# Order of the first layer's products in tiles 2 to 6 of an attention and MoE kernel

## The chip, the cores and the metric

The kernel runs on one core of a Trainium2 chip. Its time is the device time of one execution, in microseconds (us). Times given for several executions are medians. One further execution was recorded by the hardware profiler; the durations below come from it.

The engines are TensorE (PE, matrix products; PEld are its weight loads), VectorE (DVE), ScalarE (ACT), GpSimd (POOL) and SyncE (SP). Each works through its own list of instructions in order; one that needs another engine's result waits for a semaphore, and all behind it on the same engine wait too. TensorE writes to PSUM banks, here tiles of 128 x 512 f32.

## The reference

```python
q, k, v: (8, 8, 576, 64)           # batch, heads, positions, head dimension
kv  = einsum('bhsd,bhse->bhde', k, v)
out = einsum('bhsd,bhde->bhse', q, kv)
rms = sqrt(mean(out * out, axis=-1, keepdims=True) + 1e-06)
x   = (out / rms * g_norm)  as rows of 512: (4608, 512)
h   = x @ w_in                      # 512 -> 2048
g   = h * (1 / (1 + exp(-1.702 * h)))
y   = g @ w_out                     # 2048 -> 512
```

All inputs and the output are f32; the kernel multiplies in f16 and accumulates in f32.

## The kernel before, in words

**Tiles.** The 4608 rows of x are worked in nine tiles (`NT`) of 512 rows. Tiles 0 to 7 hold 512 rows of one batch each, tile 8 the 64 rows left over of every batch. The attention for tile t + 1 runs between the products of tile t's second layer, so TensorE goes from layer to layer without a pause for it. A tile's x is made by `turn` (L356): VectorE scales the rows, and a transposing DMA from SP's queue (L365) brings them to x with the columns on the partitions, in two DMAs: rows 0 to 255 of the tile (the first half of x's columns as the layers read it) and rows 256 to 511 (the second half).

**Two layers by seven products.** From tile 1 on each layer is a 2 x 2 block product done with seven block products instead of eight (Winograd's form of Strassen's method). For the first layer the weights' sums are in `ws`, made once. The sums of x are made in each tile by `Sums.form` (L505, line L509) on VectorE: four f16 arrays in the tile `xS`, 128 x 512 each. With x's quarters b11, b12 (upper half of the 512 features, first and second half of the columns) and b21, b22 (lower half), they are

- form(0): b12 - b11, "the difference of the halves", needed by product 5
- form(1): b22 - form(0), needed by product 6
- form(2): b22 - b12, needed by product 7
- form(3): b21 - form(1), needed by product 4

Products 1 and 2 use b11 and b21 only, thus only the first half of the columns. Product 3 uses b22.

**Steps.** The 16 column blocks of the hidden layer are in four groups (0 to 3). A step is written as two digits, the group and the product: "25" is product 5 of group 2. Each is four matmuls of 128 x 128 weights and 256 columns (line L577), two row blocks by two blocks of 128 features. The order of the steps is written out by hand in a `Plan`: `SECOND` (L928) for tile 1, `LATER` (L941) for tiles 2 to 6, `LAST_TWO` (L954) for 7 and 8. A group has three banks:

- x takes product 1, then adds 6, 7 and 4
- y starts as a copy of x after product 1 (the "snapshot"), then adds product 2
- z takes product 5; product 5 is also copied to `s5` in SBUF; when 5 and 6 are both done, z becomes x + s5 (an addition on VectorE, L591); then product 3 adds to z

After product 7 VectorE forms s5 = x + s5 (L593). The results y (after 2), z (after 3), s5 (after 7) and x (after 4) each go through the activation on ScalarE (`gate`, L555, line L557) into gT, the second layer's input.

`copy` (L526, line L527) makes the snapshots and the copies to s5, on the engine that the plan's `snap` names for each group: in LATER product 1 'DAAA' (group 0 on DVE, the others on ACT) and product 5 'AAAD' (groups 0, 1 and 2 on ACT). `xsums` gives the step behind which each `form` is issued, `ready` the step behind which the second layer's sums are formed.

**Order of issue.** `hid_seven` (L733) walks through the steps. A step's matmuls are issued first, then its copy or addition. The gate that a step returns is kept back, and issued behind the next step's matmuls and copies. So on ACT the gate of step n stands behind the copy of step n + 1.

**Banks.** Three pools hold the eight PSUM banks: ps_a (3), ps_h (3) and ps_o (2), lines L56 to L58. In LATER x of the groups 0 to 3 is in ps_a, ps_o, ps_o, ps_a, y always in ps_h, z in ps_a, ps_a, ps_h, ps_h. The second layer of the tile before holds both banks of ps_o until its end: one is emptied by an addition on DVE (L674), the other, the last, by a copy on ACT (L677).

Of the kernel before, what the change touches and what calls it, by code (L numbers as in the profile page):

```python
# [16 lines left out]
def kernel(  # L17
# [202 lines left out]
    class Attention:  # L220
# [3 lines left out]
        def __init__(self, b):  # L224
            self.b, self.kb = b, kvb[b] if b < EARLY else kvd[b % 2]
            self.qT, self.o = {}, {}
            x = xpool.tile([P, KO * SM], F16, name="xT", tag="xT")
            if b < EARLY:
                self.x = xT[b] = x.rearrange("p (c n) -> p c n", c=KO)
            else:  # L230
                self.x = x.rearrange("p (m r) -> p m r", r=P)
                xT[b] = x.rearrange("p (j c r) -> p c j r", j=J, c=KO)
# [65 lines left out]
        def product(self, t, c):  # L298
            nc.tensor.matmul(t, self.kb[:, c, :], self.qT[c][:, 0:SM], start=True, stop=True)  # L299
# [226 lines left out]
    def copy(engine, to, src):  # L526
        (nc.vector.tensor_copy if engine == "D" else nc.scalar.copy)(to, src)  # L527

    class SevenIn:


        def __init__(self, hid, xs, g, todo):
            self.snap = {p: e[g] for p, e in todo.snap.items()}
            self.pool = todo.pool[g]
            self.gT, self.xs, self.g, self.i = hid.gT, xs, g, PARTS[g]
            self.bank, self.done = {}, set()
            self.s5 = stage.tile([P, 2, TH], F32, name="s5", tag="s5")
# [28 lines left out]
        def product(self, p):  # L566

            name = {1: "x", 6: "x", 7: "x", 4: "x", 2: "y", 5: "z", 3: "z"}[p]  # L570
            if p in (1, 5):
                self.open(name)
            bank = self.bank
            for a in range(2):
                for k in range(KH):
                    w, x = self.operands(p, a, k)
                    nc.tensor.matmul(  # L577
                        bank[name][:, a],
                        w,
                        x,  # L580
                        start=(p in (1, 5) and a == 0 and k == 0),
                        stop=(k == KH - 1),
                        skip_group_check=True,
                    )
            self.done.add(p)
            if p == 1:
                copy(self.snap[1], self.open("y"), bank["x"])
            elif p == 5:
                copy(self.snap[5], self.s5, bank["z"])
            if p in (5, 6) and self.done >= {5, 6}:  # L590
                nc.vector.tensor_add(bank["z"], bank["x"], self.s5)  # L591
            elif p == 7:
                nc.vector.tensor_add(self.s5, bank["x"], self.s5)  # L593
                return lambda: self.gate(1, 1, self.s5)
            elif p in (2, 3, 4):
                r, n = {2: (0, 0), 3: (0, 1), 4: (1, 0)}[p]
                return lambda: self.gate(r, n, bank[name])
# [135 lines left out]
    def hid_seven(t, hid, seven, units1):  # L733
# [10 lines left out]
        for n, step in enumerate(todo.steps):  # L744
            behind, gates = gates, []
            if step != "kv":
                gate = product(step)
                if gate:
                    gates.append(gate)
            for u in behind:  # L750
                u()
            for u in units1.get(n, ()):
                u()
            for i in range(4):
                if todo.xsums[i] == n:
                    xs.form(i)
            for i0, i1, which in todo.ready.get(n, ()):
                seven.sums(i0, i1, which)
# [3 lines left out]
        def late(step):  # L762
            gate = product(step)
            if gate:
                gate()
# [144 lines left out]
    for fo in COLS[4:GROUP]:  # L910
# [28 lines left out]
        {'rows': (19, 19), 'add_up': (22, 26, 27, 31), 'table': 26, 'roots': (27, 33), 'turn': (40, 50, 51, 52)},  # L939
    )  # L940
    LATER = Plan(  # L941
# [4 lines left out]
        {1: 'DAAA', 5: 'AAAD'},  # L946
        "D",
        "aooa",
        "aahh",
        {15: '34'},  # L950
        (0, 1, 5, 10),
        {'rows': (15, 15), 'add_up': (17, 20, 24, 28), 'table': 24, 'roots': (28, 29), 'turn': (35, 38, 46, 48)},
    )
    LAST_TWO = Plan(  # L954
# [12 lines left out]
    def plan(t):  # L967
        return SECOND if t < EARLY else LATER if t < B - 1 else LAST_TWO
# [7 lines left out]
    for t in range(NT):  # L976
# [47 lines left out]
        elif b < B:  # L1024
            todo = plan(t)
# [78 lines left out]
```

## Time and profile before

| what | us |
|---|---|
| median of 3 executions | 258.92 |
| lowest and highest of them | 258.73, 259.25 |
| the profiled execution | 259.85 |
| its span, first to last instruction | 258.1 |
| PE busy in the span | 250.8 |
| DVE, ACT busy | 190.1, 180.2 |
| first layers of tiles 2, 3, 5 and 6, each | 11.80 |

The granted clock of TensorE was 1.000 of full speed over the span. In lists of groups a row gives line, engine, operation, output <- input, the count, the busy time and the mean in ns, and then the idle time of the engine in front of them with what ended it. In a timeline a row gives start and duration in us, engine, line, operation, and in brackets idle time in front. PE's rows overlap: a matmul's shown time holds its way through the array, and the next one starts before it ends. Times in the chain are start and length.

### The profile page before, as it was taken

What the parts mean: (1) busy time and instruction counts of PE and PEld (TensorE: products, weight loads), DVE (VectorE), ACT (ScalarE), POOL (GpSimd) and SP (SyncE); (2) the same over time, 40 slices, a digit from 0 to 9 for tenths busy, and PEclk for the clock granted to TensorE, in tenths of its full rate; (3) what the DMA queues carried; (4) which work ended last, traced back from release to release, by engine and by line L of the source; (5) the groups of instructions that cost most, each with busy time, mean ns of one, the idle gap of its engine ahead of it and who ended that gap; (6) DMA issues with size and microseconds to landing.
All of it is one profiled execution on the core that took longest, in us unless ns stands there. A gap on an engine that the chain in (4) does not pass through costs nothing.

```text
span 258.1 us, 6355 instructions
## 1 busy us (share of the span) xinstructions
PE 250.8 (97%) x2596; PEld 204.0 (79%) x2596; DVE 190.1 (74%) x339; ACT 180.2 (70%) x327; POOL 57.2 (22%) x91
## 2 busy tenths in 40 slices
PE   8889999999999999999899999999999999999994
PEld 2444554788888888888788888898888888888883
DVE  1565677899938794889469867986799787857872
ACT  3477725988769886988589958995899469536800
POOL 8872235116080103041160130200000000000013
PEclk9999999999999999999999999999999999999999
DMA  7999999999999986999999669986700430012005
GB/s 173 193 200 205 204 204 197 234 198 150 159 178 201 203 118 139 139 136 169 182 144 205 82 152 134 156 95 137 204 3 0 84 163 3 0 60 105 3 19 145
DMA packets 68671, 35.33 MB, mean 137 GB/s; under 512 B 37954, under 2 KB 66242, under 8 KB 68386
## 3 DMA queue, kind: packets, MB, share of 16 engines
q0 software_dynamic: 37616, 18.31, 55.6%
q1 hardware_dynamic: 30624, 16.29, 29.5%
q8 instruction: 20, 0.33, 0.5%
q10 hardware_dynamic: 402, 0.33, 0.4%
q14 instruction: 9, 0.07, 0.1%
HBM read 36.70 MB, written 9.44 MB: 179 GB/s over the span
## 4 chain that ended last, share of the span: by engine, by line
PE 89%; DMA 7%; DVE 1%; issue 0%; ACT 0%; POOL 0%; DVEq 0%
PE h L577 38%; PE o L697 36%; PE o L812 5%; PE hT L470 5%; DMA xT<-x 2%; DMA vbuf<-in_v_dram 2%; DMA qraw<-in_q_dram 2%; PE kvp L246 2%; PE outR L329 1%; PE ss L376 1%; DVE x L359 1%; PE outT L299 0%; PE q L451 0%; PE kvp L258 0%; DVE xT L386 0%
## 5 line engine op out<-in xcount | busy, mean ns | idle before, releaser
L557 ACT ACTIVATE gT<-h 128x512 f16<-128x512 f32 x96 | 52.3, 601 | 5.6 <-PE h L577 5.6
L577 PEld LDWEIGHTS <-ws 128*128 128x128 f16 x512 | 50.1, 98 | 7.0 <-issue 1.1
L577 PE MATMUL h<-xS,ws 128*128 128x256 f16 x384 | 53.0, 273 | 1.0 <-DVE xS L509 1.0
L697 PEld LDWEIGHTS <-gS 128*128 128x128 f16 x512 | 49.0, 98 | 6.2 <-DVE gS L629 0.3
L697 PE MATMUL o<-tw,gS 128*128 128x256 f16 x384 | 45.6, 273 | 0.0
L577 PEld LDWEIGHTS <-w_in_sb 128*128 128x128 f16 x384 | 37.5, 98 | 4.7
L697 PEld LDWEIGHTS <-gT 128*128 128x128 f16 x384 | 37.6, 98 | 4.3
L577 PE MATMUL h<-xT,w_in_sb 128*128 128x256 f16 x224 | 31.8, 273 | 0.0
L697 PE MATMUL o<-w_out_sb,gT 128*128 128x256 f16 x256 | 31.4, 273 | 0.0
L591 DVE TENSOR_TENSOR h<-h,s 128x512 f32<-128x512 f32 x32 | 22.3, 699 | 11.3 <-PE h L577 5.3
L674 DVE TENSOR_TENSOR osb<-o,qf 128x512 f32<-128x512 f32 (+1 forms) x25 | 16.7, 668 | 11.7 <-PE o L697 11.7
L593 DVE TENSOR_TENSOR s<-h,s 128x512 f32<-128x512 f32 x32 | 22.1, 691 | 4.4 <-PE h L577 3.3
L629 DVE TENSOR_TENSOR gS<-gT 128x512 f16<-128x512 f16 (+2 forms) x32 | 21.3, 685 | 0.6 <-ACT gT L557 0.6
L557 ACT ACTIVATE gT<-s 128x512 f16<-128x512 f32 x32 | 19.8, 628 | 2.6 <-DVE s L593 2.6
L731 POOL DMA_DIRECT2D out_dram<-osb x6 | 3.2, 540 | 82.5 <-DVE osb L674 82.5
L577 PE MATMUL h<-xS,w_in_sb 128*128 128x256 f16 x128 | 18.9, 272 | 0.0
L345 DVE TENSOR_REDUCE sum<-sq 128x8 f32<-128x512 f16 x24 | 14.9, 678 | 4.8 <-ACT sq L339 4.8
L984 ACT ACT_TABLE_LOAD x14 | 18.0, 1283 | 0.3
L317 ACT ACTIVATE sq<-outT 128x512 f16<-128x512 f32 (+1 forms) x16 | 7.8, 489 | 14.5 <-PE outT L299 8.9
L378 ACT ACTIVATE rs<-ss,eps_t 128x512 f32<-128x512 f32 (+1 forms) x16 | 9.2, 581 | 11.5 <-PE ss L376 11.4
L527 ACT COPY h<-h 128x512 f32<-128x512 f32 x27 | 15.4, 577 | 2.2 <-PE h L577 2.0
L577 PE MATMUL h<-xT,ws 128*128 128x256 f16 x112 | 16.8, 273 | 0.0
(104 smaller groups left out, 358.9 us busy)
## 6 DMA issues: line engine op xcount, KB each, us to landing
out_dram<-osb SPq DMA_DIRECT2D x8, 512.0 KB, 4.3
kraw<-in_k_dram POOLq DMA_DIRECT2D x5, 512.0 KB, 7.4
vbuf<-in_v_dram POOLq DMA_DIRECT2D x5, 512.0 KB, 10.2
out_dram<-osb SPq DMA_DIRECT2D x2, 1024.0 KB, 4.8
qraw<-in_q_dram POOLq DMA_DIRECT2D x3, 512.0 KB, 12.2
qbuf<-in_q_dram POOLq DMA_DIRECT2D x3, 512.0 KB, 6.0
out_dram<-osb SPq DMA_DIRECT2D x6, 192.0 KB, 5.7
w_in_sb<-in_moe_w_in_dram POOLq DMA_DIRECT2D x2, 512.0 KB, 9.8
```

The lines of the kernel that those rows point to most:

```text
L345: nc.vector.tensor_reduce(out=self.sum4[:, j, :], in_=self.o[j][1].rearrange("p (x d) -> p x d", d=D), op=ALU.add, axis=mybir.AxisListType.X,)
L470: nc.tensor.matmul(self.h[fo], w_in_sb[:, ko, fo * P : (fo + 1) * P], self.x[:, ko], start=(ko == 0), stop=(ko == KO - 1),)
L527: (nc.vector.tensor_copy if engine == "D" else nc.scalar.copy)(to, src)
L557: nc.scalar.activation(self.gT[:, to, n * TH : (n + 1) * TH], src, AFT.Gelu_apprx_sigmoid)
L577: nc.tensor.matmul(bank[name][:, a], w, x, start=(p in (1, 5) and a == 0 and k == 0), stop=(k == KH - 1), skip_group_check=True,)
L591: nc.vector.tensor_add(bank["z"], bank["x"], self.s5)
L593: nc.vector.tensor_add(self.s5, bank["x"], self.s5)
L629: op(s[:, n, lo], a, b)
L674: nc.vector.tensor_add(o, ps, self.kept[with_][:, m])
L697: nc.tensor.matmul(o, a, w, start=(p in (1, 2, 5) and i == 0 and (mo == 0 or split)), stop=(i == HF - 1), skip_group_check=True,)
L812: nc.tensor.matmul(os[mo], gT[:, fo, mo * P : (mo + 1) * P], w_out_sb[:, fo, :], start=(fo == 0), stop=(fo == FO - 1),)
L984: u2.setdefault(i, []).append(lambda: f(*args))
```

## The change

In the plan LATER the order of the first eight products is

- before: 21, 01, 25, 22, 05, 06, 11, 02
- after: 21, 01, 11, 22, 25, 05, 06, 02

and the rest stays. Four products (16 matmuls) that read only b11 and b21 stand before 25, the first that reads form(0); before it was two (8 matmuls). The snapshot of step 11 is not taken behind 11 but at a step of its own, written "10", between 06 and 02, so ps_h hands out its banks in the same order as before: y of group 2, y of group 0, z of group 2, y of group 1. A step with product 0 issues only the snapshot. form(1) is issued behind the first step with form(0), thus ahead of the snapshot of 01 on DVE. `ready` and the last two of `xsums` grow by one, since the plan has one step more, and mean the same places.

```diff
         def __init__(self, hid, xs, g, todo):
             self.snap = {p: e[g] for p, e in todo.snap.items()}
+            self.held = f"{g}0" in todo.steps
...
+            bank = self.bank
+            if p == 0:
+                copy(self.snap[1], self.open("y"), bank["x"])
+                return None
             name = {1: "x", 6: "x", 7: "x", 4: "x", 2: "y", 5: "z", 3: "z"}[p]
             if p in (1, 5):
                 self.open(name)
-            bank = self.bank
...
             self.done.add(p)
-            if p == 1:
+            if p == 1 and not self.held:
                 copy(self.snap[1], self.open("y"), bank["x"])
...
     LATER = Plan(
-        "21 01 25 22 05 06 11 02 15 26 03 16 12"
+        "21 01 11 22 25 05 06 10 02 15 26 03 16 12"
         " 07 31 27 13 17 35 36 04 23 24 32 33 14 37",
-        {22: ((0, 4, 0), (0, 4, 1)), 25: ((4, 6, 0),)},
+        {23: ((0, 4, 0), (0, 4, 1)), 26: ((4, 6, 0),)},
...
-        (0, 1, 5, 10),
+        (0, 0, 6, 11),
```

In the changed kernel the lines from L534 on are shifted: L557 becomes L558, L577 becomes L581, L591 and L593 become L595 and L597, and later ones grow by four.

## Prediction

> **What bounds the kernel now.** I read the page of the profile first, then TensorE's waits, then the chain that ended last, then the start of a first layer instruction by instruction. From the page:
>
> ```profile
> span 258.1 us, 6355 instructions
> PE 250.8 (97%) x2596; PEld 204.0 (79%) x2596; DVE 190.1 (74%) x339; ACT 180.2 (70%) x327; POOL 57.2 (22%) x91
> PEclk9999999999999999999999999999999999999999
> ...
> L577 PE MATMUL h<-xS,ws 128*128 128x256 f16 x384 | 53.0, 273 | 1.0 <-DVE xS L509 1.0
> ```
>
> TensorE (PE) is busy for 97% of the span at full clock. A reordering of its products can therefore win only idle time of PE, and loses whatever new idle time it makes. The list of PE's waits has one in the first layers:
>
> ```profile
> PE h L577 <- DVE xS L509: 1.0, 1, 1.0
> ```
>
> One wait in one tile, for the difference of x's halves. The chain in order of time says which tile:
>
> ```profile
> 100.41 11.80 PE h L577 x108
> ...
> 121.88 5.91 DMA xT<-x
> ...
> 128.37 11.08 PE h L577 x100
> ```
>
> It is tile 4: the second transposing DMA of its x took 5.91 us, and only then could VectorE form the difference. The changed plan, LATER, serves tiles 2 to 6, and the other four have no wait in the list. Tile 3's first layer, at 100.41, takes 11.80 us; over 108 matmuls that is 0.109 us each, so a product (4 matmuls) takes 0.437 us. The timeline of tile 3, a tile without the wait:
>
> ```profile
> 100.25 1.04 PE L577 MATMUL h<-xT,w_in_sb 128*128 128x256 f16 x8
> 100.45 0.58 ACT L677 COPY osb<-o 128x512 f32<-128x512 f32 x1 [0.52 <-PE o L697]
> ...
> 100.93 0.59 ACT L527 COPY h<-h 128x512 f32<-128x512 f32 x1
> 101.12 0.60 PE L577 MATMUL h<-xS,ws 128*128 128x256 f16 x4
> 101.33 0.70 DVE L527 COPY h<-h 128x512 f32<-128x512 f32 x1 [1.26 <-PE h L577]
> 101.58 0.60 PE L577 MATMUL h<-xT,w_in_sb 128*128 128x256 f16 x4
> 101.76 0.58 ACT L527 COPY s<-h 128x512 f32<-128x512 f32 x1 [0.24 <-PE h L577]
> 102.01 1.04 PE L577 MATMUL h<-xS,ws 128*128 128x256 f16 x8
> 102.65 0.58 ACT L527 COPY s<-h 128x512 f32<-128x512 f32 x1 [0.30 <-PE h L577]
> 102.88 1.04 PE L577 MATMUL h<-xT,w_in_sb 128*128 128x256 f16 x8
> 103.13 0.60 ACT L557 ACTIVATE gT<-h 128x512 f16<-128x512 f32 x1
> 103.27 0.70 DVE L591 TENSOR_TENSOR h<-h,s 128x512 f32<-128x512 f32 x1 [0.92 <-ACT s L527]
> 103.77 0.57 ACT L527 COPY h<-h 128x512 f32<-128x512 f32 x1
> 104.39 0.58 ACT L527 COPY s<-h 128x512 f32<-128x512 f32 x1
> 104.63 0.60 PE L577 MATMUL h<-xT,ws 128*128 128x256 f16 x4
> ...
> 109.71 3.02 ACT L557 ACTIVATE gT<-h 128x512 f16<-128x512 f32 x6
> ```
>
> Names: "25" is group 2's product 5. On PE the rows are 21 and 01 (100.25), 25 (101.12), 22 (101.58), 05 and 06 (102.01), 11 and 02 (102.88), two more, and 03, the eleventh, at 104.63. On ScalarE (ACT): the last tile's output (100.45), the snapshot of 21 (100.93), the copy of 25 (101.76), the copy of 05 (102.65), the gate of 22 (103.13), the snapshot of 11 (103.77), the copy of 15 (104.39). The DVE row at 103.27 is the addition for group 0: it needs the copy of 05 and the end of 06, and 03 accumulates onto its result. It ends at 103.97, PE comes to 03 at 104.63. A result of DVE reaches PE in 0.06 us (tile 4, below), so 0.60 us of slack is left.
>
> **The change part by part.** No instruction is added or removed; PE, ACT and DVE each run the same set in another order in five tiles, and the queues of SP and POOL keep theirs, so no DMA is issued from another place. The new order on PE is 21, 01, 11, 22, 25, 05, 06, 02, and from 02, the eighth, everything stands at its old place.
>
> *The wait in front.* 25 moves from third to fifth, so the difference has 2 x 0.437 = 0.87 us more. Only tile 4 can use it:
>
> ```profile
> 126.37 1.04 PE L577 MATMUL h<-xT,w_in_sb 128*128 128x256 f16 x8
> ...
> 127.89 0.42 DVE L509 TENSOR_TENSOR xS<-xT 128x512 f16<-128x512 f16 x1 [2.04 <-DMA xT<-x]
> ...
> 128.37 0.60 PE L577 MATMUL h<-xS,ws 128*128 128x256 f16 x4 [0.96 <-DVE xS L509]
> ...
> 131.86 0.60 PE L577 MATMUL h<-xT,ws 128*128 128x256 f16 x4
> ```
>
> Eight matmuls from 126.37 put 25 at 127.24; it ran at 128.37, which is 1.13 us lost (the row says 0.96, as modelled ends reach past the next start). The difference ends at 128.31, which gives the 0.06 us used above.
>
> *ScalarE's order, which is what I expect to decide.* Before, ACT copied 25, copied 05, then gated 22. Now 22 ends before 25, and its gate is issued behind 25's copy and ahead of 05's: copy of 25, gate of 22, copy of 05. In tile 3, 25 now ends where 05 did, so its copy starts at 102.65; the gate follows at 103.13 as before; the copy of 05 comes after the gate. How soon a copy can follow a gate no row shows alone: the snapshot at 103.77 starts 0.64 us after its gate, but it waits for that gate's bank. Six gates in 3.02 us, 0.60 the last, start 0.48 us apart, and so do the copy and gate at 102.65 and 103.13. I take 0.48, as 05's copy does not use the gate's result; 0.64 stays as the upper end. The copy of 05 then starts at 103.61 and ends at 104.19; with the 0.04 us between 103.23 and 103.27 the addition starts at 104.23 and ends at 104.93, and 03 can start at 104.99 instead of 104.63. In short, the copy of 05 is 0.96 us later against 0.60 us of slack. That is **0.36 us of new PE idle per clean tile** (0.52 at the upper end), paid in full as PE has nothing else to do: its queue goes on with 16 and 12 behind 03.
>
> A rule to hold against the 0.48: the Trainium skill, ScalarE: Activation LUTs, section What ACT_TABLE_LOAD costs, gives an ACTIVATE with immediate scale and bias 186 ns + 0.833 ns an element and lets the next overlap it by about 93 ns. For 512 elements that estimate is 0.52 us from gate to copy, hence 0.40 us a tile, 0.2 us more over five; the rows' 0.48 goes into my sum.
>
> *Tile 4 after the change.* 25 would start at 126.37 + 4 x 0.437 = 128.12 and still waits until 128.37. The second difference is now ahead of 01's snapshot on DVE; that snapshot (0.70 us, at 101.33 in tile 3) starts about 128.65, ends at 129.35 and holds 06 from 129.24 to 129.41. The ACT chain from 25 gives: copy at 129.01, gate 129.49, copy of 05 at 129.97 to 130.55, addition to 131.29, 03 at 131.35. Before it was 131.86: 0.51 us won. In clean tiles DVE has been idle for 1.26 us before the snapshot at 101.33, which covers the earlier second difference (0.41 us).
>
> *11 in third place.* Its bank of pool ps_o comes free with ACT's copy of the last tile's output, which ends at 101.03; a result of ACT reaches PE in 0.06 us (the copy that ends at 101.52, PE at 101.58), and 11 is due at 101.12. It fits by 0.03 us: cost 0, up to 0.1 a tile if the latency is worse. The snapshot of 11 moves from 103.77 to about 104.09 and the later ACT and DVE work by less than the 0.36 us that PE loses, except form(2) and the additions behind it, whose readers (07, 13, 27) come over 0.5 us later.
>
> *Sum.* Against the profiled execution: 4 x 0.36 - 0.51 = +0.93 us, 259.85 to 260.78. The median of the three runs, 258.92, is 0.93 below the profiled one, and the lowest, 258.73, is 259.85 - 1.13 almost exactly: I take it that the runs mostly lack tile 4's wait. Then all five tiles pay: 258.73 + 5 x 0.36 = 260.5. If the runs have the wait, 258.92 + 0.93 = 259.9.
>
> **The rivals.** *Faster: the late transpose is common without the profiler.* A tile with a landing like tile 4's wins 0.51 us, a clean one loses 0.36 us; it decides from three late tiles in five (-1.53 + 0.72 = -0.8 us, 258.1); five would give 256.4. For it, the landing time of this transpose varies:
>
> ```profile
> DMA to landing us min/median/max: 3.1/3.3/5.9
> ```
>
> Against it: half of the twelve landed within 3.3 us, the other four tiles have no such wait, and the median is below the profiled time.
>
> *No change: the chain through ACT is shorter than I add up*, or the difference is late in two tiles (-1.02 + 1.08, 259.0). The slack of 0.60 us would have to reach 0.9; the steps of tile 3 leave no room for that, as each is a row of its own.
>
> *Worse: a copy follows a gate only after its end, as at 103.77.* 5 x 0.52 = 2.6 us, 261.3. The bank of 11 with 0.1 us a tile would add 0.5 us to the main case, 261.0.
>
> *A clock drop.* These rows bear on what idle time does to PE's clock:
>
> ```profile
> 126.00:128.00 2.00, 1.41 (x13) 1.11 (x12) 0.11 (x1) 1.13 (x3) 0.08 (x1) 1.00 0.80 201
> 128.00:130.00 2.00, 1.63 (x15) 1.47 (x15) 1.25 (x3) 0.71 (x2) 1.99 (x4) 1.00 1.04 233
> ```
>
> The granted clock (1.00, before the DMA share) held through tile 4's gap. Were it halved by each new gap for the sixteen products behind 03, that would be 16 x 0.437 = 7.0 us a tile, 35 us in all, 294. The Trainium skill, TensorE: Matmul & The Clock Gate, section A second HAM failure mode: psum-queue depth-cycling, describes short idles between groups of matmuls re-throttling the clock; the trace contradicts it here for one gap of 0.96 us.
>
> **How the numbers follow.** New idle at 03, at 0.48 or 0.64 and with tile 4's wait or without: 0.86, with 259.5 to 261.3. No change 0.07; faster 0.06; the clock 0.01. 0.2% (0.5 us) is about what a measurement of this kernel tells from no change. So faster 0.06, same 0.07, slower 0.87. The prediction is 260.5; the range 259.4 to 261.3 leaves out the faster case, most of no change, and the clock.
>
> **What would show it.** Right: five idle times of PE at L581 released by DVE's addition L595, 0.3 to 0.5 us each, at 03; in ACT's order a gate between two copies s<-h; no wait over 0.3 us for xS. Wrong: no such wait in clean tiles (ACT's chain mis-added), PE waiting at the third product for ACT's output copy, or a time under 258.4, which would mean that xS was late in most runs of before.

## The result, and the profile after

The changed kernel takes 261.22 us (median of 6, 260.58 to 261.28), the kernel before 259.22 us (median of 6, 258.73 to 260.3, three of them new). The ratio is 1.0075, 95% interval 1.0058 to 1.0093: slower, by about 2 us. The profiled execution took 261.2 us with a span of 259.4.

The page of the changed kernel, and its list of TensorE's waits:

```profile
span 259.4 us, 6345 instructions
PE 250.5 (97%) x2596; PEld 203.6 (78%) x2596; DVE 190.3 (73%) x339; ACT 179.0 (69%) x327; POOL 57.2 (22%) x91
```

```profile
PE h L581 <- DVE h L595: 1.0, 5, 0.2
```

TensorE's work is the same, and the wait for xS (L509) is gone from the list. In its place are five waits, one for each of the tiles 2 to 6, and they are for L595, the addition that makes z of group 0. The chain in order of time through tile 3 of the changed kernel:

```profile
101.40 2.21 PE h L581 x20
103.61 0.02 issue
103.63 0.58 ACT s L527
104.22 0.50 ACT gT L558
104.72 0.49 ACT s L527
105.20 0.02 issue
105.23 0.71 DVE h L595
105.94 0.04 issue
105.98 7.58 PE h L581 x68
```

The chain used to stay on TensorE for 108 matmuls. Now it leaves TensorE after twenty (from 25's end), goes through ScalarE with the copy of 25, the gate of 22 and the copy of 05, then through VectorE's addition, and comes back to TensorE at 03. The layer ends at 105.98 + 7.58 = 113.56, thus 12.16 us long instead of 11.80: 0.36 to 0.37 us lost. The other four tiles give the same difference, the late one included. That waits of 0.2 us are listed and 0.37 us are lost is the reading that the prediction met in tile 4: a matmul's modelled end reaches past the point where the next could start.

The same place in the timeline of the changed kernel:

```profile
103.00 1.47 PE L581 MATMUL h<-xS,ws 128*128 128x256 f16 x12
103.63 0.58 ACT L527 COPY s<-h 128x512 f32<-128x512 f32 x1 [1.12 <-PE h L581]
104.11 0.60 ACT L558 ACTIVATE gT<-h 128x512 f16<-128x512 f32 x1
104.60 0.59 ACT L527 COPY s<-h 128x512 f32<-128x512 f32 x1
...
105.23 0.70 DVE L595 TENSOR_TENSOR h<-h,s 128x512 f32<-128x512 f32 x1 [2.22 <-ACT s L527]
...
105.98 0.60 PE L581 MATMUL h<-xT,ws 128*128 128x256 f16 x4 [0.20 <-DVE h L595]
```

ScalarE was idle for 1.12 us before the copy of 25. The gate of 22 could have run in that time, since 22 was done 0.44 us earlier than 25, but it stands behind the copy.

**What a profiled execution holds beside the change.** A second trace of the kernel before (the run e9_before_again) took 258.61 us, with a span of 256.8. Its chain in order of time:

```profile
46.80 9.21 PE h L577 x84
...
126.38 11.80 PE h L577 x108
```

Tile 4, at 126.38, has no wait here, and the list of TensorE's waits has none for xS. Against this trace the changed one is 2.6 us longer: five times 0.37 makes 1.85, and 0.78 us is start-up, for tile 1's first layer begins at 47.58 in the changed kernel's chain:

```profile
47.58 9.21 PE h L581 x84
```

The start-up is not the change's. Over the twelve traces of this study that point lies between 46.7 and 48.5, and in the run e4_sum_back, with the changed order of products, it is at 46.82.

### The profile page after: what moved, and what is told of

It reads as the page before. It is cut to its first block, busy times and chain, and to the rows that moved or that the text cites. A ratio compares the mean times of both kernels' runs of the same rounds, so it can differ in the third digit from the quotient of the medians.

```text
span 259.4 us, 6345 instructions
## 1 busy us (share of the span) xinstructions
PE 250.5 (97%) x2596; PEld 203.6 (78%) x2596; DVE 190.3 (73%) x339; ACT 179.0 (69%) x327; POOL 57.2 (22%) x91
## 4 chain that ended last, share of the span: by engine, by line
PE 87%; DMA 5%; ACT 3%; DVE 2%; POOL 1%; issue 1%
PE o L701 38%; PE h L581 34%; PE o L816 5%; PE hT L470 5%; DMA w_in_sb<-in_moe_w_in_dram 3%; DMA qraw<-in_q_dram 2%; ACT s L527 2%; PE kvp L246 2%; DVE h L595 1%; PE outR L329 1%; ACT gT L558 1%; PE ss L376 1%; POOL w_in_sb L180 0%; PE q L451 0%; PE kvp L258 0%
## 5 line engine op out<-in xcount | busy, mean ns | idle before, releaser
L558 ACT ACTIVATE gT<-h 128x512 f16<-128x512 f32 x96 | 52.6, 602 | 6.2 <-PE h L581 6.1
L581 PEld LDWEIGHTS <-ws 128*128 128x128 f16 x512 | 50.0, 98 | 7.7 <-issue 1.9
L581 PE MATMUL h<-xS,ws 128*128 128x256 f16 x384 | 52.2, 273 | 0.0
L581 PEld LDWEIGHTS <-w_in_sb 128*128 128x128 f16 x384 | 37.4, 98 | 4.8
L595 DVE TENSOR_TENSOR h<-h,s 128x512 f32<-128x512 f32 x32 | 22.2, 697 | 14.8 <-ACT s L527 11.1
L581 PE MATMUL h<-xT,w_in_sb 128*128 128x256 f16 x224 | 31.1, 273 | 0.0
L597 DVE TENSOR_TENSOR s<-h,s 128x512 f32<-128x512 f32 x32 | 22.1, 691 | 4.4 <-PE h L581 3.3
L558 ACT ACTIVATE gT<-s 128x512 f16<-128x512 f32 x32 | 19.8, 628 | 2.6 <-DVE s L597 2.6
L581 PE MATMUL h<-xS,w_in_sb 128*128 128x256 f16 x128 | 18.9, 273 | 0.0
L581 PE MATMUL h<-xT,ws 128*128 128x256 f16 x112 | 16.8, 272 | 1.0 <-DVE h L595 1.0
```

Source lines behind the costliest of these rows:

```text
L558: nc.scalar.activation(self.gT[:, to, n * TH : (n + 1) * TH], src, AFT.Gelu_apprx_sigmoid)
L581: nc.tensor.matmul(bank[name][:, a], w, x, start=(p in (1, 5) and a == 0 and k == 0), stop=(k == KH - 1), skip_group_check=True,)
```

## Experiments

Theory A is the prediction's: the gate of 22 between the copies of 25 and 05 on ScalarE makes the addition late for 03. Rival B is VectorE's order, in which form(1) now stands ahead of 01's snapshot. Rival C is the new order on TensorE itself, or its banks.

**e1: the gate of 22 at once.** Against the changed kernel:

```diff
                 gate = product(step)
-                if gate:
+                if gate and step in todo.soon:     # ("22",) in LATER
+                    gate()
+                elif gate:
                     gates.append(gate)
```

> The changed kernel with one thing different: in LATER the gate of step 22 is issued right behind its own matmuls, ahead of 25's copy, so no gate stands between the copies of 25 and 05 on ScalarE. Theory A (ScalarE's order: copy of 25, gate of 22, copy of 05 makes the addition late): the copy of 05 starts about 0.43 us earlier, the addition ends before TensorE comes to 03, the five waits of 0.37 us are gone; a first layer of tiles 2 to 6 takes 11.80 us; the time is about 1.9 us below the changed kernel, 258.7 to 259.2. Rival B (the second difference now ahead of 01's snapshot on VectorE delays VectorE): no change, 260.6 to 261.3. Rival C (the new order on TensorE itself, or banks): no change, 260.6 to 261.3.

Measured: 259.07 us (12 runs), 0.9994 of the kernel before, interval 0.9976 to 1.0012. No wait at 03 is left. From the timeline and, last, the chain of this run:

```profile
102.65 0.60 ACT L559 ACTIVATE gT<-h 128x512 f16<-128x512 f32 x1 [0.74 <-PE h L582]
103.15 1.07 ACT L528 COPY s<-h 128x512 f32<-128x512 f32 x2
...
104.25 0.70 DVE L596 TENSOR_TENSOR h<-h,s 128x512 f32<-128x512 f32 x1 [1.84 <-ACT s L528]
...
105.01 0.60 PE L582 MATMUL h<-xT,ws 128*128 128x256 f16 x4
```

```profile
126.92 11.80 PE h L582 x108
```

The gate now runs in the idle time, the two copies follow each other, and the addition ends at 104.95, just before TensorE's due time. The other four tiles take 11.80 us as well. The order of products, and VectorE's, are the changed ones, so B and C fall.

**e2: the copy of 05 on VectorE.**

```diff
-        {1: 'DAAA', 5: 'AAAD'},
+        {1: 'DAAA', 5: 'DAAD'},
```

> The changed kernel with the copy of 05 (group 0, product 5) on VectorE instead of ScalarE, all else the same. Theory A: VectorE is idle when 05 ends, its copy takes 0.68 us and the addition follows on the same engine, done about 0.1 us before TensorE comes to 03: no wait at 03 or one under 0.1 us a tile, 258.7 to 259.4. Rival B (VectorE's order is what is late): more work on VectorE makes it worse, over 261.3. Rival C: no change, 260.6 to 261.3.

Measured: 259.26 us (12 runs), ratio 0.9998, interval 0.9969 to 1.0027. Every first layer of tiles 2 to 6 takes 11.80 or 11.81 us. Timeline of tile 3:

```profile
103.64 0.69 DVE L527 COPY s<-h 128x512 f32<-128x512 f32 x1 [1.06 <-PE h L581]
...
104.44 0.70 DVE L595 TENSOR_TENSOR h<-h,s 128x512 f32<-128x512 f32 x1
...
105.19 0.60 PE L581 MATMUL h<-xT,ws 128*128 128x256 f16 x4
```

More work on VectorE, less on ScalarE, and the loss is gone. It was ScalarE's queue, not VectorE's.

**e3: one more instruction in front of the copy of 05.**

```diff
-        "21 01 11 22 25 05 06 10 02 15 26 03 16 12"
+        "21 01 11 22 25 10 05 06 02 15 26 03 16 12"
...
-        (0, 0, 6, 11),
+        (0, 0, 7, 11),
```

> The changed kernel with step 10 (the snapshot of 11 on ScalarE) in front of 05 instead of behind 06; TensorE's order stays. Now copy of 25, gate of 22, snapshot of 11, copy of 05 stand on ScalarE, and the snapshot waits for the gate's bank. Theory A: the copy of 05 starts 0.64 us later still, the wait at 03 grows from 0.37 to 1.0 us a tile, 3.2 us more in all: 264.4, between 263.8 and 264.9. Rivals B and C: no change within 0.3 us, 260.6 to 261.5.

Measured: 264.51 us (4 runs), ratio 1.0192, interval 1.0155 to 1.0229. Waits, then chain, of this run:

```profile
PE h L581 <- DVE h L595: 4.1, 5, 0.8
```

```profile
102.90 2.21 PE h L581 x20
...
108.11 7.58 PE h L581 x68
```

The layer takes 108.11 + 7.58 - 102.90 = 12.79 us, 0.99 us more than 11.80, where 1.0 was expected. The loss follows the place of one copy in ScalarE's queue.

**e4: form(1) back behind 01.**

```diff
-        (0, 0, 6, 11),
+        (0, 1, 6, 11),
```

> The changed kernel with the second difference, form(1), back behind step 01, so VectorE has its old order; the order of the products on TensorE and ScalarE as changed. Theory A: the wait of 0.37 us at 03 stays in each of five tiles, 260.6 to 261.3. Rival B: the waits go and the time falls to 258.7 to 259.3. Rival C: no change.

Measured: 260.67 us (10 runs), ratio 1.0048, interval 1.0029 to 1.0067. The waits are those of the changed kernel:

```profile
PE h L581 <- DVE h L595: 1.0, 5, 0.2
```

VectorE's order has no part in it, against B. The median is 0.5 us under the changed kernel's, with overlapping intervals; the traced layers are equally long, and the trace's start-up is 0.76 us shorter.

**e5: 22 ahead of 25 alone,** in the kernel before:

```diff
-        "21 01 25 22 05 06 11 02 15 26 03 16 12"
+        "21 01 22 25 05 06 11 02 15 26 03 16 12"
```

> The kernel before with one swap in LATER: 21, 01, 22, 25, 05, 06, 11, 02, so 12 matmuls stand before 25 and the snapshot of 11 stays behind 11. ScalarE has the order of the changed kernel again (copy of 25, gate of 22, copy of 05), but 25 ends one product (0.437 us) earlier than there. Theory A (it is the length of ScalarE's chain from the end of 25): the copy of 05 starts 0.53 us later than before against 0.60 us of slack, no wait at 03 over 0.05 us, the time within 0.5 us of the kernel before, 258.6 to 259.6. Rival (the gate between the copies costs its 0.37 us wherever 25 stands): waits at 03 in five tiles, 260.6 to 261.3.

Measured: 261.23 us (6 runs), ratio 1.0069, interval 1.0041 to 1.0097. I expected no loss, and the time is what the rival gave. The waits and the timeline show another cause than either:

```profile
PE h L577 <- ACT h L527: 1.4, 5, 0.3
```

```profile
102.43 0.58 ACT L677 COPY osb<-o 128x512 f32<-128x512 f32 x1 [0.52 <-PE o L697]
102.91 0.59 ACT L527 COPY h<-h 128x512 f32<-128x512 f32 x1
...
103.56 0.60 PE L577 MATMUL h<-xT,w_in_sb 128*128 128x256 f16 x4 [0.29 <-ACT h L527]
...
105.60 0.59 ACT L527 COPY s<-h 128x512 f32<-128x512 f32 x1
...
106.22 0.70 DVE L591 TENSOR_TENSOR h<-h,s 128x512 f32<-128x512 f32 x1 [1.90 <-ACT s L527]
...
107.05 0.60 PE L577 MATMUL h<-xT,ws 128*128 128x256 f16 x4
```

There is no wait for the addition L591, as theory A has it for this order. But 22 adds to y, which is 21's snapshot, and ScalarE makes that snapshot only after the last tile's output copy: it ends at 103.50, and TensorE wanted 22 in third place at 102.23 + 2 x 0.437 = 103.10. It began 0.46 us late. In both kernels 22 is fourth, where the snapshot is ready within 0.02 us of the due time; this edge I had not priced. Five times 0.46 us is 2.3 us, inside the interval of the ratio (1.1 to 2.5 us). That the time is the rival's is a coincidence. Since 22 delays everything behind it alike, the run still tests the length of the chain from 25. The gate of 22 stands between the copies of 25 and 05 here too, at 105.11; the addition ends at 106.92, and 03 starts at 107.05, eight products (8 x 0.437) behind 22 and thus without a wait. The copy of 05 starts 107.05 - 105.60 = 1.45 us ahead of 03, against 1.98 in the kernel before: 0.53 us of the 0.60 us of slack are used, as expected. So the gate between the copies does not cost 0.37 us wherever 25 stands.

**e10: 25 and 22 swapped back,** in the changed kernel; 11 stays third, and 12 matmuls stand before 25:

```diff
-        "21 01 11 22 25 05 06 10 02 15 26 03 16 12"
+        "21 01 11 25 22 05 06 10 02 15 26 03 16 12"
```

> The changed kernel with 25 and 22 swapped back: 21, 01, 11, 25, 22, 05, 06, 10, 02, so 12 matmuls stand before 25, and on ScalarE the copies of 25 and 05 follow each other, the gate of 22 behind them. 22 is fifth, long after the snapshot of 21 that held it in the run with 22 third. Theory A: the copy of 05 ends about 0.5 us earlier than in the changed kernel, no wait at 03 and no other in a first layer, 11.80 us each, 258.6 to 259.5. Rival (moving 11 to the third place, with its bank and its late snapshot, costs something itself): waits of 0.1 us or more a tile, over 259.9.

Measured: 259.41 us (10 runs), ratio 0.9999, interval 0.9975 to 1.0024; first layers of 11.79 us and no wait in them. The timeline of tile 3:

```profile
103.06 0.59 ACT L527 COPY s<-h 128x512 f32<-128x512 f32 x1 [0.67 <-PE h L581]
...
103.93 0.59 ACT L527 COPY s<-h 128x512 f32<-128x512 f32 x1 [0.29 <-PE h L581]
...
104.42 0.60 ACT L558 ACTIVATE gT<-h 128x512 f16<-128x512 f32 x1
104.55 0.70 DVE L595 TENSOR_TENSOR h<-h,s 128x512 f32<-128x512 f32 x1 [1.66 <-ACT s L527]
```

25 is one place earlier, so both copies are done before ScalarE comes to the gate, and the loss is gone without any change of the issue rule. The move of 11 with its late snapshot costs nothing.

**e9: the kernel before once more.**

> The kernel before once more, for a second trace of it. If the late transpose in front of tile 4 is a thing of that one execution, the first layers of tiles 2 to 6 take 11.80 us each with no wait for form(0); if it belongs to the kernel under the profiler, tile 4 waits about 1 us again.

Measured: 258.61 us, one execution, shown above. Its tile 4 has no wait: the late transpose was a thing of the first trace's execution.

**e6, e7, e8: x made late.** In the kernel before, the changed one and e1, the last `turn` of tiles 2 to 6 is put behind an output addition on VectorE:

```diff
-        ... 'turn': (35, 38, 46, 48)},
+        ... 'turn': (35, 38, 46, 84)},
```

> The kernel before, with VectorE's last turn of tiles 2 to 6 (j = 3) put behind the second of the output additions, so that the second half of x comes about 2.5 us later to tiles 3 to 7. Expected: TensorE waits for form(0) in front of 25 in tiles 3 to 6 and in front of product 5 in tile 7, about 0.8 us each, 4 us in all: 263.2, between 261.5 and 265.5. If x has more slack than the 1.6 us read in tile 3 the time stays under 260.

> The changed kernel with the same late turn as the one before. Theory A: a late x costs before's order 0.8 us a tile and this order next to nothing in front of 25, while the 0.37 us at 03 stay; per tile 3 to 6 it is 0.4 to 0.5 us ahead of the late kernel before, tile 7 waits as there: 1.3 to 2 us below it, about 261.5. Rival (16 matmuls in front buy nothing, the transfer or VectorE is late for another reader): the same time as the late kernel before or more.

> The same late turn in the changed kernel with the gate of 22 issued at once. Theory A: it keeps the gain in front of 25 and has no wait of 0.37 us at 03, so some 2.5 to 3.2 us below the late kernel before and 1 to 1.8 us below the late changed one, about 260.2. Rival: no difference from the late changed kernel, if the late snapshot of 01 or form(1) on VectorE takes the wait's place.

Measured: 264.97, 263.78 and 262.52 us (4 runs each), ratios to the kernel before 1.02 (1.0164 to 1.0235), 1.0179 (1.013 to 1.0227) and 1.0104 (1.0062 to 1.0146). TensorE's waits in the three, in this order:

```profile
PE h L577 <- DVE xS L509: 4.7, 5, 1.8
```

```profile
PE h L581 <- DVE xS L509: 2.1, 3, 1.0
...
PE h L581 <- DVE h L595: 0.6, 3, 0.2
```

```profile
PE h L582 <- DVE xS L509: 2.0, 3, 1.3
```

With a late x the old order waits in all five tiles after the moved turns (3 to 7), the new one in three (3, 6 and 7; the plan of 7 is the same in all). The trace of e7 has the listed wait at 03 in tiles 2, 4 and 5. Tile 4 compares the orders at equal lateness: the layer starts at 128.50 in e6 and at 127.88 in e7, and the difference, form(0), 1.01 us later in both. The difference and 25 in e6, then in e7:

```profile
129.51 0.42 DVE L509 TENSOR_TENSOR xS<-xT 128x512 f16<-128x512 f16 x1 [1.54 <-DMA xT<-x]
...
129.99 0.60 PE L577 MATMUL h<-xS,ws 128*128 128x256 f16 x4 [0.45 <-DVE xS L509]
```

```profile
128.89 0.43 DVE L509 TENSOR_TENSOR xS<-xT 128x512 f16<-128x512 f16 x1 [1.53 <-DMA xT<-x]
...
129.64 1.47 PE L581 MATMUL h<-xS,ws 128*128 128x256 f16 x12
```

The old order wanted 25 at 128.50 + 0.87 = 129.37 and lost 0.62 us; the new one wanted it at 127.88 + 1.75 = 129.63 and lost nothing in front of it. From the start of tile 1's first layer to the end, which leaves the start-up out, the traces take 263.0 - 47.15 = 215.85, 261.9 - 46.88 = 215.02 and 260.4 - 46.97 = 213.43 us. In these traces the changed order is 0.8 us ahead of the old one when x is late, less than the 1.3 to 2 us that I expected, and with the gate at once it is 2.4 us ahead, just short of the expected 2.5 to 3.2. The changed and the old late medians differ by 1.2 us, but their intervals overlap. The lateness was also larger than I had put it: the late kernel before is at 264.97, not 263.2.

No version was faster than the kernel before: e1, e2 and e10 are level with it within their intervals.

## Why the prediction was right

The forecast was slower, 260.5 us, with 259.4 to 261.3; 261.22 was measured.

- **ScalarE's order decides: right, and in its size.** 0.36 us a tile was predicted, 0.37 measured in each of five. e1, e2 and e10 take the gate or the copy out of the way by three different edits, and each removes all of it; e3 adds one instruction there and adds what it should.
- **0.48 us from a gate to the copy behind it: right.** The copy at 104.60 follows the gate at 104.11 by 0.49 us, which is nearer to the rows' 0.48 than to the estimate of 0.52 worked out from the Trainium skill's page ScalarE: Activation LUTs (section What ACT_TABLE_LOAD costs). The upper end of 0.64 was a bank's wait, as argued: in e10 a snapshot that waits for its gate's bank follows it by 105.05 - 104.42 = 0.63 us again.
- **The wait in front of 25: right as a mechanism, and seen in one of two traces of the kernel before.** The changed kernel's trace has a late x too (VectorE idle 0.82 us in front of form(0) in tile 4) and no wait. With x made late, 16 matmuls in front do shorten the wait. What it is worth in ordinary executions is too little to measure: e1 has the 16 matmuls in front of 25 and not the loss at 03, and is level with the kernel before.
- **The runs mostly lack tile 4's wait: in keeping with the second trace,** which has none; how often it comes, two traces cannot say. In the changed kernel's trace all five tiles pay.
- **Tile 4 with its late landing, forecast to win 0.51 us: right in size, where x is as late as that.** The changed kernel's own trace has no such tile. In tile 6 of e6 the difference starts 1.54 us behind the layer's start (in tile 4 of the first trace 1.52), in e7 1.83 us. The difference and 03 in e6, then in e7:

```profile
183.48 0.43 DVE L509 TENSOR_TENSOR xS<-xT 128x512 f16<-128x512 f16 x1 [2.06 <-DMA xT<-x]
...
187.45 0.60 PE L577 MATMUL h<-xT,ws 128*128 128x256 f16 x4
```

```profile
182.68 0.43 DVE L509 TENSOR_TENSOR xS<-xT 128x512 f16<-128x512 f16 x1 [2.35 <-DMA xT<-x]
...
186.15 0.60 PE L581 MATMUL h<-xT,ws 128*128 128x256 f16 x4
```

  From the difference to 03 the old order takes 3.97 us and the new one 3.47: 0.50 us won. In e7, 06 starts 0.19 us late in this tile, held by the snapshot of 01 behind form(1) on VectorE, where 0.17 was predicted. So VectorE's order has a part when x is late; in e8 the same hold is 0.20 us.
- **The base of the sum: off by half a microsecond.** I added 5 x 0.36 to 258.73, the lowest run, because it matched the profiled time less the wait. The median of six was 259.22. Start-up varies by up to 1.8 us between traces, which I had not allowed for; that this sets the medians apart is not shown. Median to median the change cost 2.0 us, against 1.85 from the traced waits. The measured time lies only 0.08 us under the upper end of the range, which stood for 0.52 us a tile. The time alone would not have told that from 0.36 us on a higher base; the traces do.
- **11 in third place: no cost,** as predicted; e10 shows it alone.
- **The clock held,** against the rival. In every window from 74 us to 206 us, where the five gaps lie, it is 1.00 in both the changed kernel and e3. A window of the changed kernel (tile 4), then one of e3, with the granted clock ahead of the last two columns:

```profile
127.00:153.00 26.00, 25.80 (x299) 22.81 (x297) 19.86 (x34) 20.45 (x41) 5.97 (x10) 1.00 1.01 153
```

```profile
129.00:156.00 27.00, 26.17 (x303) 23.17 (x301) 20.24 (x34) 21.00 (x41) 6.08 (x10) 1.00 0.96 148
```

  The prediction has the trace contradict the Trainium skill, TensorE: Matmul & The Clock Gate, section A second HAM failure mode: psum-queue depth-cycling. That was too strong: the section speaks of short idles that come frequently. One gap a tile, some 26 us apart, does not test it.

## What to carry to other kernels

Moving matmuls on an engine that never idles also moves the instructions that empty their banks on the engines beside it, and there the order of issue decides. Write down the new queue of each such engine around the moved step, and compare how much later its critical copy becomes with the slack of the matmul that reads the result; here that was 0.96 us later against 0.60 us of slack, and three small edits, each to one place of a queue, undid it. In e5 the copy that decided was another one, the snapshot of 21, so each copy that a moved step touches has to be compared. A cover against a late transfer is worth what the transfer's lateness costs in ordinary executions, and one trace with the wait does not say how often it comes.

## What the runs showed of the hardware

The start-up of this kernel differs between executions by up to 1.8 us (46.7 to 48.5 at the start of tile 1's first layer over twelve traces), nearly as much as the change. The two latest, e3 at 48.45 and e5 at 48.50, are the two in which TensorE's granted clock fell to 0.50, between 13.5 and 16.5 us; in the other ten the clock was 1.00 over the start-up and that layer began by 47.6. The fall comes long before the first moved step, and its reason stays open: the waits listed for TensorE just before it, 0.6 to 0.7 us, are no longer than in other traces. The transposing DMA of x took 5.9 us at worst in the first trace of the kernel before and 4.4 to 4.8 us at worst in the other eleven, with a median of 3.1 to 3.3 us in all. Five gaps of 0.37 us, or 1.0 us in e3, in one execution did not lower the granted clock in the windows where they lie (1.00).
